# One bank-sized PSUM pool for all stages but the last, row-paired conv halo and low-rank matmuls, and an on-chip start, in a fused conv and low-rank mixer kernel

## The chip, the cores and the metric

The kernel runs on one core of one Trainium2 chip. The metric is device time in microseconds (us), lower is better. Executions of one kernel lie within about 1% of each other. Each ratio below compares a version with the kernel before by runs taken in the same rounds on the same chip. A difference between two versions in us can cross rounds and chips; the kernel before came out at 509.1 to 510.2 us in all of them.

The engines are called PE (TensorE matmuls), PEld (its weight loads), DVE (VectorE), ACT (ScalarE), POOL (GpSimd) and SP (the queue that issues hardware DMAs).

## The reference

`x` is 8 x 4224 x 192 in float32. A causal convolution with 7 taps (softmax of a weight per head, 8 heads of 24 channels) gives `y`; then a low-rank mix over the sequence and a channel MLP:

```python
# conv: out[b,s,h,:] = sum_k softmax(weight)[h,k] * x_pad[b, s+k, h, :]
xt = y.transpose(0, 2, 1)
h = xt @ U @ V                            # U: 4224 x 32, V: 32 x 4224
u = y + h.transpose(0, 2, 1)
ch = np.maximum(u @ w_ch1, 0.0) @ w_ch2   # 192 x 768, 768 x 192
out = u + ch
```

## The kernel before

Tokens are cut into 264 tiles of 128; 8 tiles make a group, so there are 33 groups. Per group the kernel computes h, adds y (that is u), transposes u, multiplies by W1 (6 pieces `m`, each two halves in two 64-row tiles of the PE array), applies ReLU and multiplies by W2 for the group before. The conv and `tt = U.T y` of the next batch are spread between. The conv of a tile is two matmuls with a 128 x 256 "band" of taps: one over the tile itself, one over the tile before it.

PSUM is the memory that matmuls write; DVE and ACT then empty it. The kernel uses eight banks of it. Four hold W1's outputs (two tiles of two banks), two hold W2's, and the last two are a single two-bank tile `aux`, which conv, tt, h and the transposes all use in turn:

```python
h1_ps = ctx.enter_context(tc.tile_pool(name="h1_ps", bufs=2, space=bass.MemoryType.PSUM))
ch_ps = ctx.enter_context(tc.tile_pool(name="ch_ps", bufs=2, space=bass.MemoryType.PSUM))
aux_ps = ctx.enter_context(tc.tile_pool(name="aux_ps", bufs=1, space=bass.MemoryType.PSUM))

def aux_tile():
    return aux_ps.tile([P, 2, 512], F32, name="aux")

def h_piece(g, half):
    ps = aux_tile()
    for i in range(Q):
        nc.tensor.matmul(out=ps[:, i // 2, ...], lhsT=V_sb[:, j * P : (j + 1) * P],
                         rhs=tt_tiles[b][:], start=True, stop=True)
    # ... u = y + ps on DVE, two tiles at a time

# w1_piece: one two-bank tile, its first half emptied by ACT, its second by DVE
h1 = h1_ps.tile([P, 2, TOK], F32, name="h1")
# ... six matmuls ...
nc.scalar.activation(out=rl[:, m, 0:TOK], in_=h1[:, 0, :], func=ACT.Relu)
nc.vector.tensor_scalar_max(out=rl[:, m, TOK : 2 * TOK], in0=h1[:, 1, :], scalar1=0.0)
```

The order within a group is W1 m=0,1 / h / 8 tiles' worth of W2 / h / W2 / W1 m=2,3 / conv / W2 / conv / W2 / W1 m=4,5 / transposes / W2 / conv / W2.

At the start the band is made by writing a padded row of taps to DRAM and reading it back with a skewed pattern; batch 0 of x is loaded by POOL's software queue, which turns float32 into bf16 on the way.

## Time and profile before

| | us |
|---|---|
| time, median of 3 runs | 509.97 |
| span of the profiled run | 506.0 |
| PE busy | 397.8 (79%) |
| start of the first W1 matmul | 55.2 |
| first W1 to last W2 matmul | 446.1 |

The profile's page of the kernel before: busy time, share of the span and instruction count for each engine, then the chain of work that ended last.

```profile
PE 397.8 (79%) x3952; PEld 251.8 (50%) x3952; DVE 247.7 (49%) x444; ACT 215.3 (43%) x300; POOL 26.4 (5%) x37
...
PE 56%; DVE 19%; ACT 16%; DMA 5%; issue 2%; ACTq 0%; DVEq 0%
```

A third of the chain is DVE and ACT, although both are under half busy: PE waits for them somewhere. The list of waits of the kernel before (engine, tile and line, who ended the wait: us in total, times, longest) says where. L225 is h, L188 conv, L236 the addition that empties h, L299 and L300 the ReLU halves:

```profile
DVE rl L300 <- ACT rl L299: 145.4, 100, 3.0
...
PE aux L225 <- DVE u_ring L236: 42.1, 33, 1.6
...
PE aux L188 <- DMA band<-vz_d: 26.6, 1, 26.6
...
PE aux L188 <- ACT uT L256: 12.2, 14, 1.4
PE aux L188 <- ACT y_sb L174: 9.3, 24, 0.9
```

Apart from the one for the band at the start, PE's waits shown here are for `aux`: the stages need the tile again before DVE or ACT has emptied it. One of them in the timeline of the kernel before (start, duration, engine, line, operation; in brackets the idle time before it and who ended it):

```profile
311.11 0.60 ACT L299 ACTIVATE rl<-h_3281 128x512 bf16<-128x512 f32 x1 [1.25 <-PE h_3281 L269]
311.59 0.50 PE L225 MATMUL aux<-tt_sb,V_sb 128*128 128x192 bf16 x4
311.75 0.69 DVE L300 TENSOR_SCALAR rl<-h_3281 128x512 bf16<-128x512 f32 x1 [0.89 <-ACT rl L299]
...
312.95 1.01 DVE L236 TENSOR_TENSOR u_ring<-y_sb,aux 128x384 bf16<-128x384 bf16 x2
314.01 0.50 PE L225 MATMUL aux<-tt_sb,V_sb 128*128 128x192 bf16 x4 [1.26 <-DVE u_ring L236]
```

The first half of h is done before 312.1. DVE first does two ReLUs, the first of which waited for ACT, then empties aux at 313.96; only then can the second half of h start. PE stands still for 1.26 us, and so it does in nearly every group. The Trainium skill, page "Perfetto Trace Analysis", section "Optimization Strategy", says that the same gap repeating on the engine that should be saturated can mean that there is not enough SBUF or PSUM for the next tile. This trace agrees: the wait of h for `aux` stands 33 times in the list above, 42.1 us in all.

The second tool is the distance between the starts of consecutive matmuls, which gives the true price of a matmul when nothing waits (the busy time does not, as matmuls overlap: a W2 matmul counts as 246 ns busy, and the next starts 83 ns after it). In this trace it is 83 ns for W2 (192 columns), 172 ns for conv (408), 56 ns for a transpose, 214 ns for a W1 pair whose halves start 3 to 4 ns apart in two 64-row tiles. W1 to anything else takes 308 and not 213 ns, and W2 to W1 178 and not 83 ns: a change of tiling mode costs 95 ns.

### The profile page before, as it was taken

The page shows a single profiled execution, that of the slowest core. Times are in us where ns is not written, and L with a number is a line of the kernel's source. Part 1 is how long each engine was busy: PE and PEld are TensorE (multiplying, and loading weights), DVE is VectorE, ACT ScalarE, POOL GpSimd, SP SyncE. Part 2 cuts the span into 40 slices and gives each one's busy share as a digit, 9 for nine tenths or more (in the row PEclk, how much of TensorE's full clock was granted, in tenths as well). Part 3 has the DMA queues.
Part 4 walks back from the last instruction along what each step waited for, and adds up shares of the span by engine and source line. Part 5 has one row for each costly group of instructions (what it writes and reads, how often), then busy time and mean ns, then how long its engine had stood idle before and what let it go on. Part 6 is the DMA issues. An engine that isn't in the chain of part 4 may idle for free.

```text
span 506.0 us, 9221 instructions
## 1 busy us (share of the span) xinstructions
PE 397.8 (79%) x3952; PEld 251.8 (50%) x3952; DVE 247.7 (49%) x444; ACT 215.3 (43%) x300; POOL 26.4 (5%) x37
## 2 busy tenths in 40 slices
PE   0055678988888888888898888988898888899896
PEld 0022335555555555655565555555555555565555
DVE  2012444445455554644555454554464545666664
ACT  1011255544435545354544453445444543444442
POOL 9001000100100001000100001000000000000000
PEclk9999999999999999999999999999999999999999
DMA  9991901681292117721292219512121121222224
GB/s 136 204 198 13 117 1 62 93 147 49 63 167 87 48 48 113 143 63 48 54 185 63 64 48 139 115 48 63 48 79 48 48 63 49 75 68 77 81 64 126
DMA packets 76841, 43.10 MB, mean 85 GB/s; under 512 B 41344, under 2 KB 76544, under 8 KB 76672
## 3 DMA queue, kind: packets, MB, share of 16 engines
q0 software_dynamic: 39424, 14.40, 25.0%
q1 hardware_dynamic: 37376, 28.11, 18.2%
q8 instruction: 31, 0.51, 0.4%
q14 instruction: 10, 0.08, 0.0%
HBM read 29.36 MB, written 26.74 MB: 111 GB/s over the span
## 4 chain that ended last, share of the span: by engine, by line
PE 56%; DVE 19%; ACT 16%; DMA 5%; issue 2%; ACTq 0%; DVEq 0%
PE ch L310 16%; PE aux L188 8%; DVE rl L300 8%; DVE u_ring L236 6%; ACT rl L299 6%; PE aux L250 5%; ACT y_sb L174 4%; ACT rl L295 4%; PE aux L225 4%; DVE uT L255 3%; ACT uT L256 3%; DMA band<-vz_d 2%; DMA vz_d<-vz 2%; PE aux L209 2%; DVE y_sb L176 1%
## 5 line engine op out<-in xcount | busy, mean ns | idle before, releaser
L310 PE MATMUL ch<-W_sb,rl 128*128 128x192 bf16 x1584 | 158.2, 246 | 0.0
L310 PEld LDWEIGHTS <-rl 128*128 128x128 bf16 x1584 | 131.8, 98 | 15.0 <-issue 7.0
L188 PE MATMUL aux<-x_sb,band 128*128 128x408 bf16 x256 | 60.1, 361 | 52.5 <-DMA band<-vz_d 26.6
L320 DVE TENSOR_TENSOR o<-ch,u_ring 128x384 f32<-128x384 f32 x132 | 72.7, 551 | 42.3 <-PE ch L310 41.3
L269 PEld LDWEIGHTS <-W_sb 64*128 64x128 bf16 x1188 | 50.3, 94 | 64.1 <-issue 15.8
L174 ACT ACTIVATE y_sb<-aux 128x816 bf16<-128x816 f32 x60 | 51.1, 851 | 71.9 <-PE aux L188 71.9
L236 DVE TENSOR_TENSOR u_ring<-y_sb,aux 128x384 bf16<-128x384 bf16 (+1 forms) x136 | 67.1, 536 | 21.0 <-PE aux L225 21.0
L225 PE MATMUL aux<-tt_sb,V_sb 128*128 128x192 bf16 x264 | 34.2, 254 | 42.6 <-DVE u_ring L236 42.1
L188 PEld LDWEIGHTS <-band 128*128 128x128 bf16 x256 | 24.2, 102 | 82.5 <-issue 36.8
L225 PEld LDWEIGHTS <-V_sb 128*128 128x128 bf16 x264 | 18.9, 99 | 64.6 <-DVE u_ring L236 49.9
L256 ACT ACTIVATE uT<-aux 128x512 bf16<-128x512 bf16 x33 | 19.7, 597 | 25.6 <-DVE uT L255 25.6
L250 PEld LDWEIGHTS <-u_ring 128*128 128x128 bf16 x396 | 22.7, 99 | 15.1 <-issue 15.1
L250 PE MATMUL aux<-ident,u_ring 128*128 128x128 bf16 x396 | 28.4, 222 | 1.2 <-DVE u_ring L236 1.2
L255 DVE COPY uT<-aux 128x1024 bf16<-128x1024 bf16 x33 | 22.8, 692 | 4.7 <-PE aux L250 1.6
L176 DVE CAST y_sb<-aux 128x816 bf16<-128x816 f32 x4 | 4.0, 1008 | 33.3 <-PE aux L188 33.3
L71 POOL MEMSET x_sb<- 128x192 bf16 x8 | 2.0, 253 | 279.0 <-issue 246.3
L74 POOL DMA_DIRECT2D x_sb<-in_x_dram x9 | 15.2, 1692 | 1.0 <-issue 0.5
L209 PE MATMUL aux<-y_sb,U_sb 128*32 128x192 bf16 x264 | 7.9, 261 | 6.6 <-ACT uT L256 5.7
L209 PEld LDWEIGHTS <-U_sb 128*32 128x32 bf16 x264 | 6.7, 101 | 8.2 <-issue 8.2
L174 ACT ACTIVATE tt_sb<-aux 128x192 bf16<-128x192 f32 x7 | 2.3, 331 | 6.9 <-PE aux L209 6.9
L84 POOL MEMSET vz<- 128x3072 bf16 x1 | 2.7, 2685 | 0.0
L295 ACT ACTIVATE rl<-h_4833 128x1024 bf16<-128x1024 f32 x1 | 1.0, 1024 | 3.8 <-PE h_4833 L269 3.8
(548 smaller groups left out, 411.5 us busy)
## 6 DMA issues: line engine op xcount, KB each, us to landing
out_dram<-o SPq DMA_DIRECT2D x132, 192.0 KB, 2.0
x_sb<-in_x_dram POOLq DMA_DIRECT2D x7, 1584.0 KB, 15.1
W_sb<-in_moe_w_ch_dram POOLq DMA_DIRECT2D x3, 288.0 KB, 16.0
x_sb<-in_x_dram POOLq DMA_DIRECT2D x1, 816.0 KB, 8.5
V_sb<-V_sb SPq DMA_DIRECT2D x3, 264.0 KB, 7.2
x_sb<-in_x_dram POOLq DMA_DIRECT2D x1, 768.0 KB, 13.9
vz_d<-vz SPq DMA_DIRECT2D x1, 768.0 KB, 8.0
band<-vz_d SPq DMA_DIRECT2D x1, 512.0 KB, 11.4
```

Of the source, the lines that this page charges most:

```text
L174: nc.scalar.activation(out=out_ap, in_=in_ap, func=ACT.Copy)
L188: nc.tensor.matmul(out=ps[:, i, 0:CW], lhsT=band[:, h, prev * P : (prev + 1) * P], rhs=x_sb[:, s0 : s0 + HALF, h * GS : (h + 1) * GS], sta ...
L225: nc.tensor.matmul(out=ps[:, i // 2, (i % 2) * D : (i % 2 + 1) * D], lhsT=V_sb[:, j * P : (j + 1) * P], rhs=tt_tiles[b][:], start=True, st ...
L236: nc.vector.tensor_tensor(out=u_of(t0 + i + k, n), in0=in3(y_tiles[b][:, j : j + n, :]), in1=in3(ps[:, i // 2, k * D : (k + n) * D].rearra ...
L250: nc.tensor.transpose(out=ps[:, c * TOK + i * P : c * TOK + (i + 1) * P], in_=u_ring[:, r0 // 2 + i, c * P : (c + 1) * P], identity=ident[:],)
L255: nc.vector.tensor_copy(out=uT[:, 0:2, :], in_=ps[:, 0 : 2 * TOK])
L256: nc.scalar.activation(out=uT[:, 2, :], in_=ps[:, 2 * TOK : 3 * TOK], func=ACT.Copy)
L269: nc.tensor.matmul(out=h1[:, a, :], lhsT=W1_sb[rows, c, ms], rhs=uT[rows, c, :], start=c == 0, stop=c == 2,)
L299: nc.scalar.activation(out=rl[:, m, 0:TOK], in_=h1[:, 0, :], func=ACT.Relu)
L300: nc.vector.tensor_scalar_max(out=rl[:, m, TOK : 2 * TOK], in0=h1[:, 1, :], scalar1=0.0)
L310: nc.tensor.matmul(out=ch[g][:, t % 2, :], lhsT=rl_tiles[g][:, m, (t % 2) * TOK + (t // 2) * P :][:, 0:P], rhs=W2_sb[:, m, :], start=m == ...
L320: nc.vector.tensor_tensor(out=in3(o[:]), in0=in3(ch[g][:]), in1=u_of(t0, 2), op=ALU.add)
```

## The change

Its intent: let every stage but W2 draw from six single banks so that no stage waits for one tile; save PE time by running the conv's halo (only the last six rows of the tile before matter) and h as pairs in the two 64-row halves, beside W1, which is in that mode anyway; start faster by making the band with ten matmuls in place of the trip through DRAM and by loading batch 0 as three float32 chunks on the hardware queue, cast on chip. The order is rebuilt from half-groups of three W1 pieces each; the second half-group of each group also holds both halves of h for a later group ("h and h"), and in about 20 of them a conv too. The diff, cut to its core:

```diff
-    h1_ps = ctx.enter_context(tc.tile_pool(name="h1_ps", bufs=2, space=bass.MemoryType.PSUM))
+    un_ps = ctx.enter_context(tc.tile_pool(name="un_ps", bufs=6, space=bass.MemoryType.PSUM))
     ch_ps = ctx.enter_context(tc.tile_pool(name="ch_ps", bufs=2, space=bass.MemoryType.PSUM))
-    aux_ps = ctx.enter_context(tc.tile_pool(name="aux_ps", bufs=1, space=bass.MemoryType.PSUM))
+    def bank():
+        return un_ps.tile([P, 512], F32, name="un")
 # start: batch 0 in float32 chunks on the hardware queue, cast later by ACT and DVE
+    CHUNKS = [(0, 12), (12, 24), (24, NT)]
+    for a, e in CHUNKS:
+        nc.sync.dma_start(out=xf[:, a:e, :], in_=x[0, a * P : e * P, :]...)
 # start: U in long rows, transposed on chip, after chunk 1
-    nc.gpsimd.dma_start(out=U_sb[:], in_=moe_U[:].rearrange("(j p) r -> p j r", p=P))
+        if i == 1:
+            nc.vector.transpose(out=U_sb[:, 0:NU, :]..., in_=U_in[:]...)
 # start: weights and batch 1 held back until batch 0 has landed
+    nc.gpsimd.tensor_copy(out=dum[:], in_=xf[:, NT - 1, 0:1])
 # start: band from ten selection matmuls, not through DRAM (cut)
 # conv: halo pair in rows 0-63 (xh, the last six rows of each tile) and 64-127
+                k = i if halo else 1
+                src = x_tiles[b] if k else xh_tiles[b]
+                rows = slice(k * C2, (k + 1) * C2)
+                nc.tensor.matmul(out=st["ps"][i][...], lhsT=bandp[rows, h, :], rhs=src[rows, a:e, ...],
+                                 start=True, stop=False)
 # h: pairs
+                    rows = slice(i * C2, (i + 1) * C2)
+                    nc.tensor.matmul(out=ps[i][...], lhsT=V_sb[rows, ...], rhs=tt_tiles[b][rows, :], ...)
 # W1: each half has a bank and a ReLU tile of its own
+        h1 = [bank(), bank()]
 # order of one half-group k
+                for m in range(3):
+                    w1_piece(g, 3 * k + m, ("act", "dve" if k == 0 or m < 2 else "act"))
+            if k and g + 2 < NG:
+                units = [h_unit(g + 2, 0), h_unit(g + 2, 1)] + units
+            early = [u for u in units if u[0] is not None]
+            late = [u for u in units if u[0] is None]
+            late = early[3 - k :] + late if not k or len(early) < 3 else early[3:] + late
+            run(*early)          # halos and h beside W1
+            w2_piece(...)        # first half of W2
+            run(*late)           # what is left
```

## The prediction

> **What bounds it now.** Busy times of the page: PE 398 of 506 us (79%), DVE 247.7, ACT 215.3. In the timeline, matmuls that wait for nothing start at fixed distances: W2 (192 columns) 83 ns, a W1 pair in two 64-row tiles 214 ns (its two halves 4 ns apart), conv 172 ns, transpose 56 ns. Summing start distances over 60 to 486 us, 351 us are such work; about 75 us are PE standing still just before h (about 1.43 us, 31 times), conv (0.66 us, 33 times) and tt (1 us, 7 times). All three wait for the single two-bank buffer "aux" until DVE or ACT has emptied it; the list of waits shows these releasers. So the loop is PE work plus one serial buffer, about 13.1 us for each of 33 groups. The first W1 starts at 55.2 us: conv waits for the band's trip through DRAM until 26.6, then aux ping-pongs.
>
> **What changes.**
> 1. Six one-bank buffers shared by W1, conv, h, transposes: the 75 us of aux waits should go. ReLU on DVE (0.69 us) no longer waits for ACT (145 us of DVE waits listed, mostly off the path).
> 2. Conv's previous-tile matmul becomes a 64-row pair: per head four 172 ns slots become three, about 0.17 us x 56 = 10 us. h is paired too: eight slots of 83 ns become four, about 10 us in all. The Trainium skill, "TensorEngine Tiling (Array Packing)", Key Properties, says that changing tiling mode drains; this trace shows 95 ns for each change. Placing halo and h beside W1 adds almost none.
> 3. Pure PE work after, worked out from those distances: about 337 us for the loop, 10.2 us a group. DVE needs about 8.4 us a group, ACT 7.0, so neither bounds on average.
> 4. New waits, walking one half-group by hand with 0.69/0.60 us evictions: the second halo or h pair waits some 0.2 us for W1's banks; and in half-groups with h, h and one conv (about 20) the halo waits about 0.9 us, because both banks of the last W1 piece go to ACT. Together about 30 us. Loop about 367 us, 11.1 us a group.
> 5. Start: band by matmul ready near 10 us; x of batch 0 comes through the hardware queue beside U's small packets, landed near 19 us; its casts, conv, tt, h, transposes give the first W1 near 31 us. W1/W2 and batch 1 are loaded only after that: batch 1 lands near 38 us (a batch took 11.7 us from issue to last packet when alone), so the first conv of batch 1 waits a few us. Half-group 2 starts near 41 us instead of about 65.
>
> Sum: 41 + 360 + 4 us tail = 405 us of span; the timed runs stand about 3 us above the span: **408 us**, range 392 to 428, 20% faster. Chances: faster by over 2% 0.97, same 0.02, slower 0.01.
>
> **What would show it.** Step 1: gaps before h, conv, tt under 0.3 us; no wait of DVE ReLU for ACT. Step 2: halo and h matmuls starting in pairs some 4 ns apart; 83, 172, 214 ns unchanged. Step 4: the listed waits of the halo for ACT ReLU near 0.9 us; PE near 90% busy from 60 us on, DVE near 75%. Step 5: first W1 at 28 to 34 us, first halo of batch 1 waiting for a DMA until 36 to 42 us; the chain of waits mostly PE.
>
> **What would make it wrong.** A bank eviction queue on DVE or ACT that lags behind by more than my hand walk (then 415 to 430); batch 0 or its followers landing later than thought; a lower granted clock with a denser PE (1.00 in all stretches now); row-tiled halo pairs that don't run together.

## The result, and the profile after

The changed kernel takes 410.09 us (median of 4, 409.92 to 410.51) against 509.21 us of the kernel before in the same rounds. The ratio, here and below the mean time of one kernel's fast runs over that of the other's fast runs of the same rounds (so not quite the ratio of the medians), is 0.8057 with a 95% interval of 0.8032 to 0.8082: 19% faster. The predicted 408 was within 0.6%.

The page of the changed kernel, the same two parts as shown of the kernel before:

```profile
PE 376.5 (92%) x3978; PEld 248.1 (61%) x3978; DVE 286.1 (70%) x514; ACT 218.0 (53%) x412; POOL 30.4 (7%) x34
...
PE 90%; ACT 4%; DVE 4%; DMA 1%; issue 1%; DVEq 0%
```

The chain is now PE itself. In the list of waits no ReLU on DVE waits for ACT any more. No PE wait of the loop is among the 20 longest either, but that is an effect of the list: it keeps each ReLU tile apart, as `rl_1802` and so on. Added up, the halo's waits for ACT's ReLU are 7.1 us, 40 times. The busy times by stretch (stretch, length, PE, PEld, DVE, ACT, POOL busy with counts, granted clock, DMA share, GB/s) show PE at 98% in two stretches of the loop:

```profile
60.00:150.00 90.00, 87.88 (x948) 57.83 (x943) 63.87 (x114) 53.15 (x102) 5.03 (x4) 1.00 0.56 107
150.00:250.00 100.00, 97.88 (x1082) 65.11 (x1081) 70.09 (x125) 56.74 (x110) 7.53 (x6) 1.00 0.55 105
```

But not all of this is needed work. Busy time counts a matmul until its modelled end, so a wait hides in it in part. The timeline of a half-group with h, h and a conv (L301 is h, L244 the halo, L255 the conv proper, L358 and L360 ReLU):

```profile
134.30 1.89 ACT L358 ACTIVATE rl_1802<-un 128x512 bf16<-128x512 f32 x3 [1.14 <-PE un L349]
...
135.40 0.65 PE L301 MATMUL un<-tt_sb,V_sb 64*128 64x192 bf16 x8
...
136.09 0.59 ACT L358 ACTIVATE rl_1803<-un 128x512 bf16<-128x512 f32 x1
136.24 0.33 PE L244 MATMUL un<-xh_278,bandp 64*128 64x408 bf16 x1 [0.19 <-ACT rl_1802 L358]
...
136.73 0.33 PE L244 MATMUL un<-x_sb_277,bandp 64*128 64x408 bf16 x1 [0.16 <-ACT rl_1803 L358]
```

The two halos should start 3 ns apart; they start 0.49 us apart (of which the list shows 0.16 us as idle time), each as ACT empties the bank that it needs. The start of the changed kernel, in the timeline:

```profile
22.22 2.84 POOL L90 MEMSET xh_278<- 64x3264 f32 x1
...
22.56 4.67 DVE L405 STREAM_TRANSPOSE U_sb<-U_in 128x1024 bf16<-128x1024 bf16 x1
...
26.88 0.83 DVE L69 CAST x_sb_162<-xf 128x960 bf16<-128x960 f32 x1
...
27.86 0.88 PE L244 MATMUL un<-x_sb_162,bandp 64*128 64x216 bf16 x4 [5.72 <-DVE x_sb_162 L69]
...
38.02 2.97 PE L349 MATMUL un<-uT,W_sb 64*128 64x512 bf16 x18
```

The last chunk had landed at 19.5 us. Its cast waits until 26.9 behind the transpose of U on DVE, and PE waits 5.7 us for the cast.

For all versions below the trace gives two numbers that split the time: when the first W1 matmul starts, and how long it is from there to the start of the last W2 matmul. The rest (3.7 to 5.0 us) is the last output.

| version | first W1 | to last W2 | span | time | ratio to before (95%) |
|---|---|---|---|---|---|
| before | 55.2 | 446.1 | 506.0 | 509.2 | 1 |
| changed | 38.0 | 365.7 | 407.7 | 410.1 | 0.806 (0.803 to 0.808) |
| b_share3 | 40.0 | 370.4 | 415.1 | 417.8 | 0.819 (0.815 to 0.823) |
| b_splitrelu | 55.1 | 429.2 | 489.3 | 491.2 | 0.963 (0.958 to 0.967) |
| a_nopair | 39.0 | 371.5 | 414.5 | 416.3 | 0.816 (0.812 to 0.820) |
| a_banks4 | 38.7 | 408.1 | 450.8 | 453.3 | 0.889 (0.883 to 0.895) |
| a_m2dve | 38.1 | 359.9 | 402.1 | 403.8 | 0.791 (0.788 to 0.795) |
| a_convlate | 38.2 | 354.5 | 396.8 | 398.2 | 0.780 (0.776 to 0.784) |
| a_usplit | 36.5 | 365.6 | 406.2 | 408.3 | 0.800 (0.797 to 0.803) |
| a_xsw_us | 30.2 | 365.8 | 399.7 | 401.5 | 0.787 (0.784 to 0.790) |
| a_best | 30.6 | 353.6 | 387.9 | 390.1 | 0.766 (0.763 to 0.769) |
| a_best_nopair | 31.0 | 366.2 | 400.9 | 402.8 | 0.791 (0.787 to 0.794) |
| a_banddram | 52.9 | 365.7 | 422.8 | 425.5 | 0.835 (0.832 to 0.838) |

All versions gave correct results.

### The profile page after: what moved, and what is told of

Its sections match the earlier page's. It is cut to its first block, busy times and chain, and to the rows that moved or that the text cites. A ratio compares the mean times of both kernels' runs of the same rounds, so it can differ in the third digit from the quotient of the medians.

```text
span 407.7 us, 9513 instructions
## 1 busy us (share of the span) xinstructions
PE 376.5 (92%) x3978; PEld 248.1 (61%) x3978; DVE 286.1 (70%) x514; ACT 218.0 (53%) x412; POOL 30.4 (7%) x34
## 4 chain that ended last, share of the span: by engine, by line
PE 90%; ACT 4%; DVE 4%; DMA 1%; issue 1%; DVEq 0%
PE un L349 33%; PE ch L370 33%; PE un L255 7%; PE un L329 6%; PE un L244 5%; PE un L301 4%; PE un L275 2%; DVE U_sb L405 1%; DMA w_sb<-in_weight_dram 1%; DVE sm L160 1%; DVE u_ring L312 0%; ACT rl_476 L358 0%; DVE x_sb_162 L69 0%; ACT x_sb_162 L67 0%; PE un L180 0%
## 5 line engine op out<-in xcount | busy, mean ns | idle before, releaser
L349 PE MATMUL un<-uT,W_sb 64*128 64x512 bf16 x1188 | 140.6, 379 | 0.0
L67 ACT ACTIVATE y_sb<-un 128x408 bf16<-128x408 f32 (+2 forms) x124 | 54.1, 501 | 31.2 <-PE un L255 30.9
L312 DVE TENSOR_TENSOR u_ring<-y_sb,un 128x384 bf16<-128x384 bf16 (+1 forms) x136 | 64.5, 537 | 3.3 <-PE un L301 0.6
L335 ACT ACTIVATE uT<-un 128x512 bf16<-128x512 bf16 x33 | 19.7, 597 | 23.6 <-PE un L329 22.7
L329 PE MATMUL un<-ident,u_ring 128*128 128x128 bf16 x396 | 28.6, 221 | 1.1 <-DVE u_ring L312 1.1
L244 PEld LDWEIGHTS <-bandp 64*128 64x128 bf16 x136 | 11.0, 99 | 26.3 <-issue 17.6
L255 PEld LDWEIGHTS <-band 128*128 128x128 bf16 x136 | 10.2, 103 | 25.5 <-issue 22.5
L244 PE MATMUL un<-x_sb_162,bandp 64*128 64x408 bf16 (+2 forms) x48 | 14.2, 372 | 10.1 <-DVE x_sb_162 L69 7.4
L334 DVE COPY uT<-un 128x1024 bf16<-128x1024 bf16 x33 | 22.5, 681 | 0.8 <-PE un L329 0.8
L301 PE MATMUL un<-tt_sb,V_sb 64*128 64x192 bf16 x264 | 21.6, 246 | 1.1 <-DVE tt_sb L287 1.1
L301 PEld LDWEIGHTS <-V_sb 64*128 64x128 bf16 x264 | 15.1, 94 | 10.9 <-issue 1.7
L255 PE MATMUL un<-x_sb_162,band 128*128 128x408 bf16 (+2 forms) x72 | 17.8, 367 | 0.0
L255 PE MATMUL un<-x_sb_277,band 128*128 128x408 bf16 x64 | 15.0, 340 | 0.0
L244 PE MATMUL un<-x_sb_277,bandp 64*128 64x408 bf16 x32 | 10.6, 331 | 1.7 <-ACT rl_1986 L358 0.2
L244 PE MATMUL un<-xh_278,bandp 64*128 64x408 bf16 x32 | 9.5, 331 | 2.3 <-ACT rl_476 L358 0.4
```

Source lines behind the costliest of these rows:

```text
L67: nc.scalar.activation(out=out_ap, in_=in_ap, func=ACT.Copy)
L244: nc.tensor.matmul(out=st["ps"][i][:, 0 : (e - a) * GS], lhsT=bandp[rows, h, :], rhs=src[rows, a:e, h * GS : (h + 1) * GS], start=True, st ...
L255: nc.tensor.matmul(out=ps[:, 0 : (e - a) * GS], lhsT=band[:, h, :], rhs=x_tiles[b][:, a + 1 : e + 1, h * GS : (h + 1) * GS], start=False, ...
L301: nc.tensor.matmul(out=ps[i][:, k * D : (k + 1) * D], lhsT=V_sb[rows, j * P : (j + 1) * P], rhs=tt_tiles[b][rows, :], start=True, stop=True,)
L312: nc.vector.tensor_tensor(out=u_of(t0 + 2 * i + k, n), in0=in3(y_tiles[b][:, j : j + n, :]), in1=in3(ps[i][:, k * D : (k + n) * D].rearran ...
L329: nc.tensor.transpose(out=ps[c // 2][:, (c % 2) * TOK + i * P : (c % 2) * TOK + (i + 1) * P], in_=u_ring[:, r0 // 2 + i, c * P : (c + 1) * P],
```

## The experiments

The theory of the prediction: the serial aux tile costs 75 us of the loop, the pairs save 20 us of PE work, new bank waits give back 30, and the on-chip start saves the rest. Rivals: the gain comes from the coupling of DVE to ACT (145 us of listed waits), from the new order, or from the pairs.

### b_share3: only the sharing, in the kernel before

```diff
-h1_ps = ... tile_pool(name="h1_ps", bufs=2, ...)
-aux_ps = ... tile_pool(name="aux_ps", bufs=1, ...)
+h1_ps = ... tile_pool(name="h1_ps", bufs=3, ...)
-    return aux_ps.tile([P, 2, 512], F32, name="aux")
+    return h1_ps.tile([P, 2, 512], F32, name="two")
-    h1 = h1_ps.tile([P, 2, TOK], F32, name="h1")
+    h1 = h1_ps.tile([P, 2, 512], F32, name="two")
```

> The kernel before with one edit: its single two-bank aux buffer and its two two-bank W1 buffers become one pool of three two-bank buffers; order, start, row use and eviction stay. Theory (the serial aux buffer costs about 75 us of TensorE standing still, and any second buffer in line removes it): 435 to 455 us, the gaps before h and before conv (1.43 and 0.66 us before) mostly under 0.3 us. Rival (the gain needs single banks, the new order or paired rows): 485 us or more.

Measured: 417.8 us. The same six banks, as three two-bank tiles that all stages but W2 take in turn, give 92 of the 99 us. It beat the theory's own range. From first W1 to last W2 the trace has 370.4 us against 446.1: 75.8 us less, which is the wait that was read from the trace before. h now follows W2 at about 80 ns in 29 of 30 cases, and conv in all 32. In the timeline of b_share3 (L224 is h, L309 W2, L235 the addition that empties h), the second half of h starts before DVE begins to empty the first:

```profile
236.91 0.50 PE L224 MATMUL two<-tt_sb,V_sb 128*128 128x192 bf16 x4
...
237.25 0.82 PE L309 MATMUL ch<-W_sb,rl 128*128 128x192 bf16 x8
237.91 0.49 PE L224 MATMUL two<-tt_sb,V_sb 128*128 128x192 bf16 x4
...
238.27 1.93 DVE L235 TENSOR_TENSOR u_ring<-y_sb,two 128x384 bf16<-128x384 bf16 x4
```

The other 15 us came from the start, to which the prediction had given no price here: the conv of batch 0 also used aux. In the timeline of the kernel before, the first conv pieces after the band had landed:

```profile
26.59 1.54 PE L188 MATMUL aux<-x_sb,band 128*128 128x408 bf16 x4 [26.59 <-DMA band<-vz_d]
...
29.23 1.52 PE L188 MATMUL aux<-x_sb,band 128*128 128x408 bf16 x4 [1.10 <-DVE y_sb L176]
...
31.68 1.52 PE L188 MATMUL aux<-x_sb,band 128*128 128x408 bf16 x4 [0.94 <-ACT y_sb L174]
```

and the same stage with three buffers, all 32 matmuls in one run of 7.3 us, and the first W1:

```profile
26.77 7.32 PE L187 MATMUL two<-x_sb,band 128*128 128x408 bf16 x32 [26.77 <-DMA band<-vz_d]
...
40.04 2.52 PE L268 MATMUL two<-uT,W_sb 64*128 64x512 bf16 x12 [0.78 <-DVE uT L254]
```

In this version DVE's ReLU still waits for ACT's, and PE's distances show no cost of it. In the list of waits of b_share3:

```profile
DVE rl L299 <- ACT rl L298: 110.8, 100, 2.1
```

The rest of the loop's gain in the changed kernel is small: 365.7 against 370.4 us. Its pairs alone are worth 5.8 us of the loop (a_nopair below), so the single banks and the new order together gained nothing there beyond the sharing. (With the halo's wait removed they do gain: without pairs, a_best_nopair below has 366.2 us.) No run took the two apart.

### b_splitrelu: only the coupling of DVE to ACT removed

```diff
-h1 = h1_ps.tile([P, 2, TOK], F32, name="h1")                       # bufs=2
+h1 = [h1_ps.tile([P, TOK], F32, name="h1") for _ in range(2)]      # bufs=4
-nc.scalar.activation(out=rl[:, m, 0:TOK], in_=h1[:, 0, :], func=ACT.Relu)
-nc.vector.tensor_scalar_max(out=rl[:, m, TOK : 2 * TOK], in0=h1[:, 1, :], scalar1=0.0)
+nc.scalar.activation(out=rl[0][:, m, :], in_=h1[0][:], func=ACT.Relu)
+nc.vector.tensor_scalar_max(out=rl[1][:, m, :], in0=h1[1][:], scalar1=0.0)
```

> The kernel before with one edit: each two-bank W1 buffer becomes two one-bank buffers and the ReLU output two tiles, so that VectorE's ReLU no longer waits for ScalarE's; aux stays single. Theory (that wait matters only as far as it delays the emptying of aux by VectorE, some 0.5 us in each of 33 groups): 490 to 500 us. Rival A (the 145 us of VectorE waits are the main cost): 460 us or less. Rival B (wholly off the path): 507 to 511 us.

Measured: 491.2 us, as the theory has it. (The edit also turns ACT's one ReLU over both banks of every third piece into two, which the cut above leaves out.) The distance from W2 to the second half of h falls from about 1.51 to 0.92 us, as DVE reaches the emptying of aux earlier. So of 145 us of listed waits 17 to 18 mattered, and only through aux.

### a_nopair: the changed kernel without pairs

```diff
-                k = i if halo else 1
+                k = 1
-                    rows = slice(i * C2, (i + 1) * C2)     # in h
+                    rows = slice(0, C2)
```

> The changed kernel with halo and h matmuls all in one row half, so that the same matmuls run one after the other and not in pairs; results are unchanged. Full price by start distances: 56 x 0.172 us + 31 x 4 x 0.083 us = 20 us. Theory (in the 20 half-groups with h, h and a conv the halo waits for ScalarE's ReLU until a fixed time, which hides the longer h and part of the halo): 419 to 424 us. Rival (price paid in full): 428 to 432 us. Rival (pairing buys nothing): 410 us.

Measured: 416.3 us, 6.2 us slower: under the theory's range, 6 of the 20 us. The start distances show the hiding that it expected. Unpaired, the distances among h matmuls grow by 5.3 us and those among halos by 3.4, but those from h to the halo behind it shrink by 3.3, as the halo waits for the bank anyway. The loop grows by 5.8 us. a_best_nopair below takes this up again.

### a_banks4: four banks in the pool

```diff
-un_ps = ... tile_pool(name="un_ps", bufs=6, ...)
+un_ps = ... tile_pool(name="un_ps", bufs=4, ...)
-late = early[3 - k :] + late if not k or len(early) < 3 else early[3:] + late
+late = early[2:] + late if not k else early[3:] + late
```

> The changed kernel with four banks in the shared pool in place of six (at most two conv units open at once, so the half-group with three starts the third late). Theory (the gain is the depth of the pool): by a hand walk with 0.60 and 0.69 us evictions each half-group waits 1.1 to 1.5 us more, 66 times: 480 to 510 us, nearly all of the gain gone. Rival (order, paired rows and start make the gain): 430 us or less.

Measured: 453.3 us (two runs). The direction holds: two banks fewer cost 42 us of the loop with start, order and pairs left as they are (but for the one half-group with three conv units). The size was wrong: 0.65 us for each of 66 half-groups (43.2 / 66) and not 1.1 to 1.5. In the trace the start distances that grew sit at two places: within W1 (once per half-group 0.41 or 0.47 us in place of 0.21, and further pairs 0.07 or 0.14 us apart; 24 us in all) and within h (0.49 and 0.63 us, 31 us in all). Distances before the halo and h shrank by 15 us. The hand walk seems to have put every late eviction on PE's path; that was not tested.

### a_m2dve and a_convlate: the halo's wait for ACT

a_m2dve gives the second half of the third W1 piece to DVE where a conv rides along. a_convlate issues that conv after the first half of W2:

```diff
 # a_m2dve
+both = k == 1 and not any(w == "conv" for w, _, _ in work.get(2 * g + k, []))
-    w1_piece(g, 3 * k + m, ("act", "dve" if k == 0 or m < 2 else "act"))
+    w1_piece(g, 3 * k + m, ("act", "act" if both and m == 2 else "dve"))
 # a_convlate
-late = early[3 - k :] + late if not k or len(early) < 3 else early[3:] + late
+late = early[3 - k :] + late
```

> The changed kernel, but in half-groups with h, h and a conv the third W1 piece's second half is emptied by VectorE and not by ScalarE. The profile after shows the second halo starting 0.49 us behind the first there, 19 times. Theory (it waits for ScalarE to empty two banks one after the other): that distance falls to a few ns, 9 us less, 400 to 404 us. Rival (VectorE, at 70% busy, then delays h and the output): 408 us or more.

> The changed kernel, but in half-groups with h and h the conv is issued after the first half of W2 and not beside W1. It pays one more change into and out of 64-row mode (0.19 us), and its banks are long empty by then. Theory: 0.35 + 0.49 - 0.19 = 0.65 us less, 19 times: 397 to 400 us. Rival (the wait only moves to the next W1, because ScalarE then empties conv's banks later): 406 us or more.

Measured: 403.8 and 398.2 us, both inside the theory's ranges. In a_m2dve none of the 19 distances of about 0.49 us between two halos is left, but they are now 0.13 us and not a few ns, and the loop gains 5.7 us and not 9; the 0.43 us before the first halo stays. In a_convlate both are gone, for one more change of tiling mode in and out. In its timeline h goes straight to W2 (L370), and the two halos then start together:

```profile
133.23 0.65 PE L301 MATMUL un<-tt_sb,V_sb 64*128 64x192 bf16 x8
133.81 1.16 PE L370 MATMUL ch<-W_sb,rl 128*128 128x192 bf16 x12
134.91 0.34 PE L244 MATMUL un<-xh,bandp 64*128 64x408 bf16 x1
134.91 0.34 PE L244 MATMUL un<-x_sb,bandp 64*128 64x408 bf16 x1
```

So "placing the halo beside W1", which saves 0.19 us of mode changes, cost 0.84 us of waiting each time, since W1 had just taken all six banks.

### a_usplit: U's transpose in four pieces

```diff
+            if i < 2:
+                q = slice((2 * i + h // 4) * 8, (2 * i + h // 4 + 1) * 8)
+                nc.vector.transpose(out=U_sb[:, 0:NU, q]..., in_=U_in[:, :, q]...)
-        if i == 1:
-            nc.vector.transpose(out=U_sb[:, 0:NU, :]..., in_=U_in[:]...)
```

> The changed kernel with U's one VectorE transpose of 4.67 us, which stands before the last cast of batch 0, cut into four pieces placed in VectorE's idle times of the first two chunks. Theory (it delays the last chunk's conv and all that follows by 4.5 us, until batch 1's landing at 40.5 us becomes the limit): first W1 near 33.5 us, time 405 to 407 us. Rival (the start is limited by loads): 409 to 411 us.

Measured: 408.3 us, first W1 at 36.5 us: between the two, a miss in size. The pieces did move into DVE's idle times (1.29 to 1.31 us each). But the cast that should then have run at once met another obstacle, in the timeline of a_usplit:

```profile
22.57 3.71 DVE L69 CAST x_sb<-xf 128x960 bf16<-128x960 f32 x1
22.92 2.84 POOL L90 MEMSET xh<- 64x3264 f32 x1
```

The cast took 3.71 us where it took 0.83 us in the changed kernel, and it ended a little after POOL's memset did. Those 2.9 us are nearly the whole of the miss (36.5 us where the theory had 33.5). The Trainium skill, page "SBUF — State Buffer", section "Who interferes with whom", says that DVE and GpSimd share a port pair as an exclusive lock, and that copies, casts and `tensor_scalar` can enter the modes that take it. These traces agree: in the changed kernel a `tensor_scalar` on 8 elements takes as long as the memset beside it lasts, and in a_xsw_us, where no memset runs then, 0.17 us. The changed kernel:

```profile
5.28 2.81 POOL L90 MEMSET xh_163<- 64x3264 f32 x1
...
5.56 2.56 DVE L160 TENSOR_SCALAR sm<-sm 128x8 f32<-128x8 f32 x1
```

and a_xsw_us:

```profile
4.66 0.17 DVE L164 TENSOR_SCALAR sm<-sm 128x8 f32<-128x8 f32 x1
```

The kernel before shows it too (1.92 us), and so does a_banddram (2.10 us for the `tensor_scalar`, 1.78 us for the first cast of x). Not everything on DVE is held. In a_xsw_us the memsets, moved, run beside casts from PSUM and pieces of U's transpose, which take about as long as elsewhere (two such casts 0.94 us, a piece 1.31):

```profile
16.02 5.60 POOL L87 MEMSET xh<- 64x3264 f32 x2
...
17.44 1.27 DVE L402 STREAM_TRANSPOSE U_sb<-U_in 128x256 bf16<-128x256 bf16 x1
18.36 0.99 DVE L69 CAST y_sb<-un 128x288 bf16<-128x288 f32 x2
```

So the memset beside it is not why U's whole transpose is slow either: in a_banddram, with no memset beside it, it took 4.66 us. No run moved the memsets alone, so this cause is read from five traces, not tested by itself.

### a_xsw_us: batch 0 by the software queue again

```diff
-    for a, e in CHUNKS:
-        nc.sync.dma_start(out=xf[:, a:e, :], in_=x[0, a * P : e * P, :]...)
+    for a, e in CHUNKS:
+        nc.gpsimd.dma_start(out=x_tiles[0][:, 1 + a : 1 + e, :], in_=x[0, a * P : e * P, :]...)
-        copy("act", x_tiles[0][:, 1 + a : 1 + m, :], xf[:, a:m, :])
-        copy("dve", x_tiles[0][:, 1 + m : 1 + e, :], xf[:, m:e, :])
-    nc.gpsimd.tensor_copy(out=dum[:], in_=xf[:, NT - 1, 0:1])
     # the memsets of xh moved behind the weights' loads; U's transpose in four pieces, one chunk later
```

> The changed kernel with batch 0 loaded as before, by the software queue straight to bf16 in three chunks ahead of U, V, W1, W2 and batch 1 (no float32 chunks, no casts, no hold on the weights), and U's transpose in four pieces during the last two chunks. Theory (by the packet rate of before, 504 rows a us, the chunks are there by 7, 10 and 13 us, and W and batch 1 come earlier): first W1 at 29 to 32 us, 398 to 403 us. Rival (the float32 chunks on the hardware queue are what makes the start fast): 408 us or more.

Measured: 401.5 us, first W1 at 30.2 us. The chunks landed at 8.7, 11.8 and 14.2 us by the software queue; on the hardware queue as float32, at twice the bytes written and beside U's loads, at 9.8, 15.4 and 19.5 us, and they still had to be cast. Against a_usplit this start is 6.3 us earlier (36.5 to 30.2). A part of that is the memsets' move (2.9 us at the last cast, 2.4 us at the `tensor_scalar` before the band, not all of it on PE's path), so the price of the chunks alone is not isolated; but nothing shows a gain from them.

### a_banddram: the band through DRAM again

```diff
+    vz_d = dram.tile([P, ROW], BF16, name="vz_d")
+    nc.scalar.dma_start(out=vz_d[:], in_=vz[:].rearrange("p h t -> p (h t)"))
+    nc.scalar.dma_start(out=band[:], in_=<skewed read of vz_d>)
+    nc.scalar.dma_start(out=bandp[...], in_=<skewed read of vz_d>)   # twice, 64 rows each
-    # selection of taps, ten matmuls, four copies
```

> The changed kernel with the band made as before by a trip through DRAM (on ScalarE's queue) in place of the ten matmuls; the rest stays. Theory (band there near 27 us or later, three chunks of conv at 4.2 us each still to do, none of it overlapping the loads any more): first W1 at 44 to 48 us, 416 to 422 us. Rival (the loads and U's transpose set the start, the band's way does not matter): 409 to 412 us.

Measured: 425.5 us, first W1 at 52.9 us: 15 us slower, more than the theory's 6 to 12. The part of the band that batch 0 needs was there at 27.1 us, when the first conv ran (12.2 us in the changed kernel), and everything behind it shifted by the whole 15 us, because conv, casts and U's transpose run one after the other. In the timeline of a_banddram:

```profile
27.13 1.14 PE L225 MATMUL un<-x_sb,bandp 64*128 64x288 bf16 x4 [27.13 <-DMA bandp<-vz_d]
```

(The casts on ACT also stood behind the band's issues in ACT's queue here.) So the band by matmul works; but b_share3, with the band through DRAM, batch 0 in bf16 and U read directly, has its first W1 at 40.0. The new start as a whole gains 2 us over that: what the band saves, the float32 chunks and U's transpose nearly eat.

### a_best and a_best_nopair: the two fixes together, with and without pairs

a_best joins a_convlate and a_xsw_us and loads V and U ahead of the second chunk, with U's transpose pieces one step earlier:

```diff
+    load_chunk(*CHUNKS[0])
+    nc.gpsimd.dma_start(out=V_sb[0:R, :], in_=moe_V[:])
     # ... U_in ...
+    for c in CHUNKS[1:]:
+        load_chunk(*c)
-            if i > 0:
+            if i * 2 + h // 4 in (1, 2, 3, 4):
```

> Conv after the first half of W2 where h and h come first, batch 0 by the software queue in bf16, and U and V ahead of the second chunk so that U's transpose pieces fall into VectorE's idle times one step earlier. Theory (the two fixes add up, and U's earlier transpose takes away the 1.6 us that tt waited for it): first W1 at 28 to 29 us, then the 354.5 us from first W1 to last W2 that the late conv alone showed: 387 to 391 us. Rival (they share the same slack): 395 us or more.

Measured: 390.1 us (388.9 to 391.2, 5 runs), 4.9% under the changed kernel. The two fixes add up: 353.6 us from first W1 to last W2, as with the late conv alone. First W1 is at 30.6 and not at 28 to 29: U no longer waits, but the last chunk, queued behind V and U, now lands at 20.4 us and not at 14.2, and PE waits 1.95 us for it, in the timeline of a_best:

```profile
20.43 0.90 PE L252 MATMUL un<-x_sb,bandp 64*128 64x216 bf16 x4 [1.95 <-DMA x_sb<-in_x_dram]
```

That part of the edit bought nothing. The page of a_best shows how little is left outside PE:

```profile
PE 371.1 (96%) x3978; PEld 246.9 (64%) x3978; DVE 281.1 (72%) x514; ACT 214.9 (55%) x409; POOL 32.7 (8%) x36
...
PE 93%; DMA 4%; POOL 1%; DVE 1%; ACT 1%; issue 0%; POOLq 0%
```

a_best_nopair is a_best with the edit of a_nopair.

> The same kernel with halo and h matmuls all in one row half, so that none run as pairs. In the changed kernel unpairing cost only 6 us. Theory (there waits for banks hid it; with those waits gone the price by start distances is due, 56 x 0.172 + 31 x 4 x 0.083 = 20 us): 404 to 411 us. Rival (pairing itself is worth 6 us): 393 to 397 us.

Measured: 402.8 us. The pairs are worth 12.7 us here, against 6.2 us in the changed kernel. So waits had hidden half of it, as the theory says; but it is still not the 20 us of the sum. The start distances of a_best say where the rest went. Of the 56 halo pairs 15 start 0.13 to 0.16 us apart, almost as far as two single ones (0.172). In the second half of h, the third of the group's four pairs starts 0.13 us apart in place of 3 ns and the fourth some 0.08, so that this half takes about as long as four single matmuls. Added up over the trace, unpairing lengthens the distances among halos by 6.8 us and those among h matmuls by 5.3, 12.1 of the 12.7 us; the full price would be about 10 and 10. Both kinds of broken pair follow W1 pieces of which ACT empties one bank and DVE the other, so these coming free a little apart is the likely cause; that reading was not tested by a run of its own.

## Why the prediction was right, and where its parts were not

The total was right, 408 predicted and 410.1 measured, and so was the mechanism of the main term, but several terms were mis-sized in opposite directions.

- **"the 75 us of aux waits should go"** (step 1): right. b_share3, which changes nothing else, takes 75.8 us off the loop. The gaps before h and tt are gone; the gap before conv is gone where no half-group with h, h and conv is concerned.
- **ReLU waits "mostly off the path"**: right; b_splitrelu shows 17 to 18 of 145 us.
- **"about 10 us in all" each for halo and h** (step 2): mis-sized. Start distances of pairs were as predicted (3 to 4 ns, and 83, 172 and 214 ns unchanged), but unpairing costs 6.2 us in the changed kernel and 12.7 us where no halo waits for ACT. Step 2 priced every pair as formed; a pair whose halves start 0.13 us apart isn't. Step 4 had booked some of this loss, as 0.2 us of wait for the second pair.
- **"the halo waits about 0.9 us"** (step 4): right; 0.35 + 0.49 us, 19 times, and a_convlate, which pays 0.19 us to avoid it, gains 11 us in the loop. The walk's total for the loop, 367 us, stands against 365.7 from first W1 to last W2, but its parts cancelled: summed from start distances, the waits are about 24 us (17 before and between those halos, 7 in broken pairs) and not 30, and what remains is 342 and not 337.
- **"first W1 near 31 us"** (step 5): wrong by 7 us; it was 38.0. The landing of batch 0 (19 predicted, 19.5 measured) and of batch 1 (38 and 40.5) were close. The missing term is U's transpose on DVE: it took 4.67 us, had no number in the sum, and stood before the last cast. The other 2.3 us are not accounted for. Batch 1's 2.5 us have a plain source: the 11.7 us that the prediction took for a batch "from issue to last packet" run, in the trace of the kernel before, from the first packet to the last, and the first starts 2.5 us after the issue. Also "first halo of batch 1 waiting for a DMA" did not happen: batch 1 had landed 4 us before its first halo, which waited for ACT. The third half-group began at 45.7 and not at 41 us.
- **Where the start's gain comes from** was wrong too, though the sum did not show it: the prediction names the ping-pong on aux but gives it no price, and credits the on-chip band and the loads. The shared pool alone moves the first W1 from 55.2 to 40.0 us, as batch 0's conv had also ping-ponged on aux; the new start adds 2 us.

The late start (4.7 us) and the loop after it (about 362 us to the end of the span, 364 predicted) partly cancelled, so a total within 0.6% was partly luck. What stays open: why four banks cost less than the hand walk, why the pairs break (a likely cause, untested), and what single banks and the new order are worth by themselves.

## What to carry to other kernels

Where several stages share one PSUM tile and PE shows the same gap in every iteration, first let them share the buffers of a stage that has two; here a few lines gave 93% of a rewrite's gain, and start distances of matmuls, not busy shares, showed what the gap was worth. When work is put beside another stage to save mode changes, count the banks: a stage that has just taken all of them makes its neighbour wait for their emptying, and a row pair saves its full price only if both halves can start at once. In the start, price every instruction of the chain from a record, since a faster part (the band) can be eaten by one unpriced transpose and by a load path with more bytes.

## What the Trainium skill lacked or had wrong

- Page "TensorEngine Tiling (Array Packing)", Key Properties, says that a change of tiling mode drains the array, without a price. Here it is 95 ns each way (308 against 213 ns, 178 against 83 ns).
- The same page says that tiles operate independently. It lacks that a pair placed right behind a stage that used all banks may not start together: here up to 0.16 us lay between the halves in place of 3 ns, and all pairs gained 12.7 us in place of 20.
- Page "Vector Engine (DVE) Microarchitecture Reference", section 3.8, says that the 32 x 32 transpose sustains one element per cycle per lane. The transpose of U, 128 x 1024 bf16 with strided reads and writes of 2-byte elements, took 4.67 us, 4.6 ns for each element of a lane (1.3 us for 256). Whether the strides cause it was not tested; a memset on POOL beside it does not (4.66 us without one).
- Page "DMA: Bandwidth & Descriptors", section "Anatomy of one DMA — SWDGE (gpsimd) path", gives 2.0 us plus bytes over 436 GB/s. By the bytes read, a batch of x (3.24 MB read as 4224 rows of 768 bytes, 1.62 MB written) would take 9.4 us, an estimate from that page; in the kernel before, issued at 46.5 us with no other load in flight, it landed at 61.2, 14.7 us. Its first packet started 2.5 us after the issue, and at its steadiest the software queue moved about 504 such rows a us. The number of rows alone does not set this rate: U's 64-byte rows went at up to some 1900 a us in the same trace.
